# One expert weight loaded in four steps further back in the DMA queue, and 24 products of zeros in the TensorE order of a fused attention and mixture-of-experts kernel

## The chip, the cores and the metric

The kernel runs on one NeuronCore of a Trainium2 chip. The metric is the device time of one execution in microseconds (us); lower is better. One execution was also recorded by the hardware profiler.

## The reference

Three stages follow each other. The first is an attention over 4 batches, 8 heads, 576 tokens and 64 numbers per head; heads 0 to 3 see a local window of 32 tokens, heads 4 to 7 a stride of 32. The second sends each token to one of 8 experts (two matrix products each); whether a token takes a fresh expert or that of the token before it is decided by a gate. The third is a mixture of 4 causal attentions.

```python
# stage 1, per head
mask_local = (rel >= 0) & (rel < 32)
mask_strided = (rel >= 0) & (pos[None, :] % 32 == pos[:, None] % 32)
attn = softmax(where(mask, q @ k.T / 8, -1e9));  x = attn @ v
# stage 2, per token s
e = argmax(x @ w_gate) if s == 0 or sigmoid(x @ w_local) < 0.5 else prev_e
x = softmax(x @ w_gate)[e] * (relu(x @ w1[e]) @ w2[e])
# stage 3
out = sum over the top 2 of 4 experts of w * (softmax(causal(q @ k.T / 8)) @ v) @ wo
```

## The kernel before, in words

The change lies in the first attention, the first 130 us of some 586. Its work is cut into 16 units: unit `n` is batch `n // 4` and head pair `n % 4` (pairs 0 and 1 local, 2 and 3 strided). A unit passes through these steps:

- `load_qk(b, a)` and `load_vl` / `load_vs` (L223, L238, L243): DMA loads of queries, keys and values, all issued by SyncE (SP). Each of the nine `load_vl(b, t)` brings the local values of one stretch of tokens; it writes over the batch before, and so waits for that batch's last product with them.
- `prep` (L342): TensorE transposes `raw` into one of four rotating PSUM banks (`bank`, tag `t`), ScalarE copies it out as `ql`, `kl`, `qs`, `ks`.
- `s_mm` (L367): scores into the one PSUM tile `s`; VectorE takes the maximum (L391) and subtracts it (L397), which frees `s` for the next unit; ScalarE takes the exponential (L398).
- `et`, `pv`, `xt` (L403, L425, L465): transposes of the exponentials, product with the values, transposes of the result. `logits` and `route...` then choose the experts, batch by batch.

Beside it the weights of expert 0 are prepared: `load_w1(0)` (L159) issues four DMAs of 512 KB into `w1raw`, and sixteen `split_w1` (L165) each cut a quarter of one of the four pieces into a high part (ScalarE, L118) and a low part (VectorE, L119). They are first used by `h_early`, at the very end of this stage. `xt_early(r)` transposes rows of routed tokens that GpSimd gathers (`gather`, L187, tile `xg`).

The order is a list. `ev` collects the steps, each with a due time; it is sorted by due time and then traversed in the order of the index list `ORD`. TensorE executes exactly in that order (`manual_schedule`). SP's DMAs come out in that order too (so they stand in the trace). The orders of ScalarE, VectorE and GpSimd are made when the program is built, by a scheduler that starts an instruction when its own estimate of times says its inputs are there; every engine then executes its own list strictly in order.

`warm(n)` (L714) issues `n` products of a tile of zeros, `wz`, into a rotating bank that nobody reads; the kernel has one call of it, `warm(14)`, before the first step. `wz` shares its memory (tag `ess`, one buffer) with the strided units' exponentials.

Around the places that change the order is, before:

```python
# prep(0,1,1,0)  s_mm(1)  prep(0,2,0,0)  prep(0,2,0,1)  prep(0,3,1,1) ...
# load_qk(2,3)  s_mm(6)  load_qk(2,2)  ...  logits(0)  load_w1(0)  ...  pv(5)
# load_vl(2,0)  load_vl(2,7)  load_vl(2,2) ... load_vl(2,8) ... load_vl(2,6) ...
# s_mm(7) prep(2,0,1,0) prep(2,3,0,0) pv(6,0) prep(2,0,0,1) prep(2,2,1,0) ...
# load_qk(3,0) ... load_vs(2,2) ... load_vs(2,3) ... load_qk(3,1)
# pv(15,0)  et(15,1)  gather(0)  xt_early(0)  ...  xt_early(1)  ...  h_early(0)
```

Of the kernel before, what the change touches and what calls it, by code (L numbers as in the profile page):

```python
# [11 lines left out]
BF = mybir.dt.bfloat16  # L12
# [19 lines left out]
TAB = [{'et': [[[2.950979077143747, 3.950979077143747], [2.280661623723043, 3.280661623723043], [2.0962247253607327, 2.822324310858445], [2.6, 3.6], [2.6, 3.6]], [[3.5322171299090326, 4.532217129909033], [2.6, 3.6], [4.889421810674059, 5], [4.101973494858811, 5], [2.4273110594636376, 3.4273110594636376]]], 'pv': [[11.653333607501414, 13.276081673478151], [12.552811228649597, 12.274068241409006]], 'out': [27.06785727905669, 26.413251600982292, 31.393508979283784, 31.29028612353765, 33.51756297275431], 'load': 3.2539096467048427, 'fill': [-0.0001, 0.0, 2.2, 3.2, 3.8000000000000003, 4.7, 5.6000000000000005, 7.123278008936126, 7.475699072531977, 8.299999999999999, 9.28929322986803, 10.1, 11.279614409352465, 11.740498658223936, 13.41245718764738, 13.869517990637926, 14.180425775785736, 14.180525775785735, 16.109400886459948], 'ord': [[0, 1, 2, 3, 4], [4, 1, 3, 2, 0]]}, {'et': [[[2.6, 3.6], [0.4005259343533014, 1.4005259343533014], [2.7601240952552226, 3.7601240952552226], [1.8795577765734173, 2.8795577765734173], [4.194527945253478, 5]], [[3.136537199573193, 4.136537199573193], [2.570838837611794, 3.570838837611794], [3.583354236171958, 4.5833542361719575], [2.6, 3.6], [2.6, 3.6]]], 'pv': [[12.13577290663916, 14.511270833899513], [12.55, 12.576465944615482]], 'out': [24.42, 25.42, 27.908127481497882, 27.42, 28.42], 'load': 4.3618195128701025, 'fill': [0.2, 0.4539916075210759, 0.4540916075210759, 0.4541916075210759, 3.8000000000000003, 7.0225821487593425, 7.022682148759342, 7.022782148759342, 7.4, 8.299999999999999, 9.2, 10.1, 11.0, 11.9, 12.799999999999999, 13.60305564719335, 13.60315564719335, 13.60325564719335, 14.503255647193349], 'ord': [[0, 1, 2, 3, 4], [0, 1, 2, 3, 4]]}]  # L32
ORD = [5, 2, 0, 4, 7, 1, 3, 8, 10, 6, 16, 11, 12, 22, 19, 14, 20, 13, 17, 9, 18, 21, 24, 25, 26, 23, 29, 27, 15, 31,
# [12 lines left out]
NORM = [[[0, 1], [0, 0]], [[1, 0], [0, 0]], [[0, 1], [0, 0]], [[0, 1], [0, 0]], [[0, 0], [1, 1]]]  # L46

EE = ["avava", "vavav"]
# [8 lines left out]
def kernel(  # L57
# [18 lines left out]
    B, H, S, D = q.shape  # L76
# [16 lines left out]
    def pool(c, name, bufs=1, **kw):  # L93
        return c.enter_context(tc.tile_pool(name=name, bufs=bufs, **kw))
# [61 lines left out]
    wpool = pool(wctx, "wts")  # L156
    RAW1, RAW2, W1, W2 = {}, {}, {}, {}

    def load_w1(e):  # L159
        for c in range(4):  # L160
            t = wpool.tile([128, F], FT, name="w1raw", bufs=4)
            nc.sync.dma_start(t, moe_w1[e, c * 128:(c + 1) * 128, :])
            RAW1[e, c] = t
# [23 lines left out]
    def gather(e, rs=range(RC), rows=NT):  # L187
        for r in rs:
            t = wpool.tile([128, DM], FT, name="xg", bufs=6)
            nc.gpsimd.indirect_dma_start(out=t, out_offset=None, in_=xd[:rows],  # L190
                                         in_offset=bass.IndirectOffsetOnAxis(ap=gidx[:, r, e:e + 1], axis=0))
            XG[e, r] = t
# [10 lines left out]
    wk = pool(actx, "awk")  # L203
    ac = pool(actx, "acst")
# [8 lines left out]
    SL = (15.59, 17.66, 17.67, 17.5)  # L213
# [32 lines left out]
                nc.sync.dma_start(vs[a - LOC][64 * g:64 * g + 36, h, :, :64],  # L246
                                  dap(v, ((b * H + 2 * a + h) * S + 8 * g) * D, [[16 * D, 36], [D, 8], [1, D]]))

    wz = wk.tile([128, 512], BF, name="wz", tag="ess", bufs=1)
    nc.vector.memset(wz, 0.0)  # L250
    load_qk(0, 0)
    load_qk(0, 1)
# [148 lines left out]
    ess = {}  # L401
# [320 lines left out]
    ev = [(-9, prep, (0, a, x, hf)) for a in range(LOC) for x in range(2) for hf in range(2)]  # L722
# [26 lines left out]
    for b in range(B):  # L749
# [2 lines left out]
        r = [(logits, (b, (0, 1))), (logits, (b, (2, 3)))]  # L752
        r += [(f, (b,)) for f in (route0, route1, route_w, route2, route2b, route3, route3b, route_r, route4)]
        ev += [(o + x, *y) for x, y in zip(t, r)]
    ev += [(SL[0], slots, (slice(0, 2), slice(0, 1), lambda: gather(0, [0, 1], (B - 1) * S))), (6, load_w1, (0,))]
    for c in range(4):
        for i in range(4):
            ev.append((7.66 + W1S * (4 * c + i), split_w1, (0, c, 4, i)))
# [4 lines left out]
           (SL[2], slots, (slice(0, RC), slice(1, NE), lambda: gather(1)))]  # L763
    for f in range(8):
        ev += [(HE[f], h_early, (f,)), (YT_[f], y_early, (f,))]
    ev.sort(key=lambda x: x[0])
    for i in ORD or range(len(ev)):
        ev[i][1](*ev[i][2])
# [306 lines left out]
    def next_w(e, r):  # L1075
        for c in range(4):
            if c % RC == r or (r == 0 and c == 3):
                split_w1(e, c)

    load_w1(1)  # L1080

    ov = cst.tile([128, 4, NE], FT)
# [39 lines left out]
    xt_expert(1)  # L1122
    tc_m = ExitStack()
    load_w1(2)
    tc_m.enter_context(tc.manual_schedule(engines={mybir.EngineType.PE, mybir.EngineType.Pool}))
    load_cn(1)
# [263 lines left out]
    def qk_steps(b, pr):  # L1390
        return [(c_qk, (b, pr, n, hf)) for n in range(2) for hf in range(2)]
# [8 lines left out]
    ev = [(-4, c_t, (0, 4))] + [(-3, f, a) for f, a in qk_steps(0, 0)] + [(-2, c_v, (0, t)) for t in range(5)] + [(-1, c_top2, (0,))]  # L1400
# [54 lines left out]
```

## Time and profile before

| | us |
|---|---|
| median of 3 runs | 589.42 (586.23 to 590.1) |
| the profiled execution | 587.65 |
| its span, first to last instruction | 585.6 |
| TensorE busy | 553.1 (94% of the span) |
| VectorE busy | 383.3 (65%) |
| ScalarE busy | 348.0 (59%) |
| mean granted TensorE clock | 0.981 |

The device time holds 2.05 us beside the span. PE is TensorE's matmuls and transposes, PEld its weight loads (they overlap), DVE is VectorE, ACT ScalarE, POOL GpSimd, SP SyncE; SPq is SP's queue of DMA issues. L347 is line 347 of the kernel. The granted clock is a share of 2.4 GHz: 1.00 is the full level, 0.50 the lower one, 1.2 GHz. "Issue" as the end of a wait means that the profile shows nothing for which the engine waited.

### The profile page before, as it was taken

The numbers are of one execution on the slowest core, as the hardware profiler recorded it, in microseconds if no ns is written. First come the engines' busy times: TensorE is split into PE (matmuls) and PEld (weight loads), VectorE is DVE, ScalarE is ACT, GpSimd is POOL, SyncE is SP. The second block draws the span as 40 slices with busy tenths as digits, with TensorE's granted clock in tenths as the row PEclk, the third lists the DMA queues.
The fourth block names the chain that finished last, engine by engine and source line by source line (L and its number), as shares of the span: only waits on it lengthen the run. The fifth ranks groups of instructions, "written<-read, shape, count | busy, mean of one in ns | idle before, by whom it ended". The sixth has DMA issues, their size and how long they took to land. (4 is left out here: it accounts for less than half of the span.)

```text
span 585.6 us, 14138 instructions
## 1 busy us (share of the span) xinstructions
PE 553.1 (94%) x5207; PEld 478.4 (82%) x5207; DVE 383.3 (65%) x1145; ACT 348.0 (59%) x865; POOL 142.4 (24%) x231
## 2 busy tenths in 40 slices
PE   5999899879998999999999999998999999999996
PEld 3777778668778898988989987797987999889764
DVE  4356588855573646474747476157998888798892
ACT  4566676741373544564646467245877876776882
POOL 6032213250431432423443453220000001000000
PEclk9799699989999999999999999999999999999999
DMA  9999969640584764275837360324103402301312
GB/s 180 188 245 230 257 168 225 208 152 0 176 293 150 222 219 167 84 213 194 261 135 256 126 211 21 100 79 119 36 11 73 162 3 58 82 34 42 103 31 90
DMA packets 81127, 82.01 MB, mean 140 GB/s; under 512 B 56840, under 2 KB 57096, under 8 KB 80528
## 3 DMA queue, kind: packets, MB, share of 16 engines
q1 hardware_dynamic: 72768, 64.92, 39.7%
q0 software_dynamic: 8112, 15.76, 8.4%
q8 instruction: 59, 0.97, 0.7%
q14 instruction: 28, 0.23, 0.1%
q10 hardware_dynamic: 160, 0.13, 0.1%
HBM read 61.89 MB, written 21.76 MB: 143 GB/s over the span
## 5 line engine op out<-in xcount | busy, mean ns | idle before, releaser
L196 POOL DMA_INDIRECT yd<-y,sidx x47 | 51.2, 1089 | 91.7 <-ACT y L974 54.4
L1275 ACT ACTIVATE E<-cs,c_mx 128x288 f32<-128x288 f32 (+4 forms) x96 | 45.7, 481 | 13.8 <-DVE c_mx L1273 6.5
L122 PE MATMUL yp<-w2h,h 128*128 128x512 f32 x128 | 51.1, 399 | 0.1
L119 DVE TENSOR_TENSOR w1l<-w1raw,w1h 128x1024 fp32r<-128x1024 f32 (+1 forms) x44 | 41.5, 981 | 14.0 <-ACT w1h L118 14.0
L124 PE MATMUL yp<-w2h,h 128*128 128x512 f32 x128 | 50.0, 390 | 0.0
L123 PE MATMUL yp<-w2l,h 128*128 128x512 f32 x128 | 49.9, 390 | 0.0
L119 DVE TENSOR_TENSOR w2l<-w2raw,w2h 128x512 fp32r<-128x512 f32 x56 | 35.7, 685 | 19.2 <-ACT w2h L118 18.6
L118 ACT ACTIVATE w1h<-w1raw 128x1024 fp32r<-128x1024 f32 (+1 forms) x44 | 33.8, 832 | 19.7 <-PE hp L123 19.7
L1305 POOL MEMSET E<- 128x128 f32 x40 | 8.2, 210 | 145.9 <-PE cet L1324 69.7
L710 DVE SCALAR_TENSOR_TENSOR h<-hp,h 128x384 fp32r<-128x384 f32 x48 | 24.7, 551 | 28.8 <-ACT h L709 22.5
L118 ACT ACTIVATE w2h<-w2raw 128x512 fp32r<-128x512 f32 x56 | 31.8, 632 | 19.2 <-PE yp L124 8.2
L1268 PE MATMUL cs<-qkt 128*128 128x288 f32 (+4 forms) x192 | 39.1, 319 | 0.5 <-DVE qkt L1198 0.5
L1273 DVE TENSOR_REDUCE c_mx<-cs 128x1 f32<-128x288 f32 (+4 forms) x80 | 37.8, 483 | 1.7 <-PE cs L1268 1.0
L122 PE MATMUL qkp<-y,cw 128*128 128x288 f32 x128 | 38.7, 303 | 0.0
L124 PE MATMUL qkp<-y,cw 128*128 128x288 f32 x128 | 37.7, 295 | 0.0
L123 PE MATMUL qkp<-y,cw 128*128 128x288 f32 x128 | 37.6, 294 | 0.0
L709 ACT ACTIVATE h<-hp 128x384 fp32r<-128x384 f32 x48 | 21.4, 489 | 20.8 <-PE hp L124 13.5
L122 PE MATMUL hp<-xo,w1h 128*128 128x320 f32 (+2 forms) x96 | 30.5, 318 | 1.5 <-issue 1.5
L190 POOL DMA_INDIRECT xg<-xd,gidx x24 | 25.2, 1052 | 26.2 <-DVE gidx L653 19.2
L1319 PE MATMUL cet<-idf,E 128*128 128x128 f32 x160 | 28.2, 278 | 2.4 <-ACT et L115 0.8
L124 PE MATMUL hp<-xo,w1l 128*128 128x320 f32 (+2 forms) x96 | 30.1, 314 | 0.0
L123 PE MATMUL hp<-xo,w1h 128*128 128x320 f32 (+2 forms) x96 | 30.1, 314 | 0.0
(372 smaller groups left out, 1675.8 us busy)
## 6 DMA issues: line engine op xcount, KB each, us to landing
w1raw<-in_moe_w_dram SPq DMA_DIRECT2D x32, 512.0 KB
w2raw<-in_moe_w_dram SPq DMA_DIRECT2D x56, 256.0 KB
qkt<-qkt SPq DMA_DIRECT2D x8, 576.0 KB
yr<-yd SPq DMA_DIRECT2D x16, 256.0 KB
out_dram<-co SPq DMA_DIRECT2D x16, 256.0 KB
raw<-in_q_dram SPq DMA_DIRECT2D x16, 144.0 KB
raw<-in_k_dram SPq DMA_DIRECT2D x16, 144.0 KB
raw<-in_q_dram SPq DMA_DIRECT2D x8, 288.0 KB
```

The source lines that it names most:

```text
L118: nc.scalar.activation(hi, src, AF.Copy)
L119: (eng or nc.vector).tensor_tensor(lo, src, hi.bitcast(FT), op=OP.subtract)
L122: nc.tensor.matmul(o, ah, bh, start=start, stop=False, **kw)
L123: nc.tensor.matmul(o, ah, bl, start=False, stop=False, **kw)
L124: nc.tensor.matmul(o, al, bh, start=False, stop=stop, **kw)
L190: nc.gpsimd.indirect_dma_start(out=t, out_offset=None, in_=xd[:rows], in_offset=bass.IndirectOffsetOnAxis(ap=gidx[:, r, e:e + 1], axis=0))
L196: nc.gpsimd.indirect_dma_start(out=yds[n], out_offset=bass.IndirectOffsetOnAxis(ap=ix(n), axis=0), in_=y, in_offset=None, bounds_check=yds ...
L710: nc.vector.scalar_tensor_tensor(lo, p, 0.0, hi.bitcast(FT), op0=OP.max, op1=OP.subtract)
L1268: nc.tensor.matmul(o[:, h - h0], T[:, h, q0:q0 + 128], T[:, 2 + 2 * x + h, k0:k1], start=x == 0, stop=x == 1, skip_group_check=True)
L1273: nc.vector.tensor_reduce(mx[:, n, h0:h0 + G], o, axis=AX.X, op=OP.max, negate=True)
L1275: nc.scalar.activation(E[:, h, k0:k1], o[:, h - h0], AF.Exp, bias=mx[:, n, h:h + 1], accum_out=sm[:, n, h:h + 1])
L1319: nc.tensor.transpose(p[:, kt * 128:kt * 128 + 128], E[:, kt * 128:kt * 128 + 128], idf)
```

## The change

Three things are changed.

- `load_w1(0)`, one step that issued all four DMAs, becomes four steps of one DMA each. They stand further back: the first behind `load_vl(2,8)`, the second behind `load_vl(2,6)` (the last of the third batch's local values), the third behind `load_qk(3,0)`, the fourth behind `load_vs(2,3)`. `load_qk(2,2)`, which stood ahead of the weight, goes behind `load_vl(2,0)` and `load_vl(2,7)`.
- Four calls of `warm` are put into the order: `warm(10)` ahead of `s_mm(1)`, `warm(5)` behind it, `warm(3)` between `pv(15,0)` and `et(15,1)`, `warm(6)` ahead of `xt_early(0)`.
- `wz` gets memory of its own, since it is now read through the whole stage.

All other steps keep their places relative to each other; the index list is longer because the step list is.

```diff
-    def load_w1(e):
-        for c in range(4):
+    def load_w1(e, cs=range(4)):
+        for c in cs:
...
-    wz = wk.tile([128, 512], BF, name="wz", tag="ess", bufs=1)
+    wz = ac.tile([128, 512], BF, name="wz")
...
-    ev += [(SL[0], slots, (slice(0, 2), slice(0, 1), lambda: gather(0, [0, 1], (B - 1) * S))), (6, load_w1, (0,))]
+    ev += [(SL[0], slots, (slice(0, 2), slice(0, 1), lambda: gather(0, [0, 1], (B - 1) * S)))]
+    ev += [(6 + c * .01, load_w1, (0, (c,))) for c in range(4)]
...
+    ev += [(0, warm, (10,)), (0, warm, (5,)), (0, warm, (3,)), (0, warm, (6,))]
```

The four places in the order after, with new steps in angle brackets:

```python
# prep(0,1,1,0)  <warm(10)>  s_mm(1)  <warm(5)>  prep(0,2,0,0) ...
# load_vl(2,0)  load_vl(2,7)  <load_qk(2,2)>  load_vl(2,2) ... load_vl(2,8)
# <load_w1 0>  load_vl(2,6)  <load_w1 1>  load_qk(3,0)  <load_w1 2>
# load_vs(2,2)  load_vs(2,3)  <load_w1 3>
# pv(15,0)  <warm(3)>  et(15,1)  gather(0)  <warm(6)>  xt_early(0)
```

## Rows read from the trace of the kernel before

**Rows 1.** The page: span, and TensorE's busy time, share and instructions.
```profile
span 585.6 us, 14138 instructions
...
PE   553.1 (94%) x5207; PEld 478.4 (82%) x5207; DVE 383.3 (65%) x1145; ACT 348.0 (59%) x865; POOL 142.4 (24%) x231
```
**Rows 2.** Windows: length, busy us of PE, PEld, DVE, ACT, POOL; clock, DMA share, GB/s.
```profile
320.00:340.00 20.00, 20.00 (x140) 18.19 (x139) 10.97 (x19) 10.59 (x20) 9.24 (x9) 1.00 0.43 146
```
**Rows 3.** Windows, as in rows 2: a stretch at the lower clock.
```profile
22.00:23.00 1.00, 1.00 (x10) 1.00 (x9) 0.00 (x0) 0.85 (x3) 0.00 (x0) 0.50 0.80 167
```
**Rows 4.** Timeline of PE, first units: start, us, ..., what ended the idle time.
```profile
14.31 0.98 PE L374 MATMUL s<-ml,idb 128*128 128x480 bf16 x2 [2.93 <-DVE z L397]
...
17.03 1.03 PE L347 MATMUL prep<-idf,raw 72*128 72x72 f32 x8
19.36 0.97 PE L347 MATMUL prep<-idf,raw 72*128 72x72 f32 x12 [1.30 <-DMA raw<-in_k_dram]
```
**Rows 5.** Timeline of PE, around the longest wait.
```profile
56.72 0.56 PE L452 MATMUL pv<-vs,ess 64*64 64x65 f32 x18
60.67 0.70 PE L452 MATMUL pv<-vs,ess 64*36 64x65 f32 x14 [3.39 <-issue]
61.30 2.18 PE L347 MATMUL prep<-idf,raw 96*128 96x96 f32 x14
63.41 1.14 PE L452 MATMUL pv<-vs,ess 64*64 64x65 f32 x32
64.48 0.18 PE L560 MATMUL pk<-idb,r_row 5*128 5x5 bf16 x1
...
68.98 0.60 PE L474 MATMUL xt<-idf,xr 128*128 128x128 f32 x4
```
**Rows 6.** Windows, as in rows 2: a wait with its fall of the clock.
```profile
59.00:60.00 1.00, 0.00 (x0) 0.00 (x0) 0.00 (x0) 0.00 (x0) 0.00 (x0) 0.50 1.02 397
```
**Rows 7.** Timeline of PE: steps of the same form at the full clock.
```profile
36.57 0.89 PE L379 MATMUL s<-kl,ql 64*64 64x96 f32 x31 [0.59 <-issue]
37.39 0.72 PE L347 MATMUL prep<-idf,raw 96*128 96x96 f32 x7
37.95 0.51 PE L481 MATMUL xt<-idf,xs 100*128 100x100 f32 x4
...
39.23 0.69 PE L452 MATMUL pv<-vs,ess 64*64 64x65 f32 x32
39.85 0.72 PE L347 MATMUL prep<-idf,raw 96*128 96x96 f32 x7
```
**Rows 8.** DMA queues in 34.0:34.1: packets, MB, share of 16 engines.
```profile
q8 instruction: 1, 0.02, 64.7%
```
**Rows 9.** DMA queues in 58.0:58.1.
```profile
q8 instruction: 1, 0.02, 71.6%
```
**Rows 10.** Timeline of SPq: DMA issues.
```profile
11.48 0.39 SPq L230 DMA_DIRECT2D raw<-in_k_dram  x1
...
49.70 3.10 SPq L162 DMA_DIRECT2D w1raw<-in_moe_w_dram  x4
53.36 0.59 SPq L240 DMA_DIRECT2D vla<-in_v_dram  x1
...
78.14 0.48 SPq L230 DMA_DIRECT2D raw<-in_q_dram  x1
```
**Rows 11.** Windows, as in rows 2: the last load of rows 10 runs out.
```profile
83.00:84.00 1.00, 1.00 (x15) 0.94 (x11) 0.86 (x6) 0.56 (x3) 0.00 (x0) 1.00 0.52 133
```
**Rows 12.** Timeline of PEld: weight loads of the products of zeros.
```profile
3.73 0.15 PEld L717 LDWEIGHTS <-wz 128*128 128x128 bf16 x1 [0.28 <-issue]
4.11 1.18 PEld L717 LDWEIGHTS <-wz 128*128 128x128 bf16 x6 [0.23 <-issue]
```
**Rows 13.** Timeline of PE: the end of the first attention.
```profile
127.82 0.63 PE L671 MATMUL xpe<-idf,xg 128*128 128x128 f32 x4 [1.27 <-DMA xg<-xd,gidx]
```
**Rows 14.** Waits of ACT in 0:180.
```profile
ACT w2s L118 <- DMA w2e<-in_moe_w_dram: 0.9, 1, 0.9
```

More of the change, by code (lines that the diff above doesn't have):

```diff
@@ L32 @@
 TAB = [{'et': [[[2.950979077143747, 3.950979077143747], [2.280661623723043, 3.280661623723043], [2.0962247253607327, 2.822324310858445], [2.6, 3.6], [2.6, 3.6]], [[3.5322171299090326, 4.532217129909033], [2.6, 3.6], [4.889421810674059, 5], [4.101973494858811, 5], [2.4273110594636376, 3.4273110594636376]]], 'pv': [[11.653333607501414, 13.276081673478151], [12.552811228649597, 12.274068241409006]], 'out': [27.06785727905669, 26.413251600982292, 31.393508979283784, 31.29028612353765, 33.51756297275431], 'load': 3.2539096467048427, 'fill': [-0.0001, 0.0, 2.2, 3.2, 3.8000000000000003, 4.7, 5.6000000000000005, 7.123278008936126, 7.475699072531977, 8.299999999999999, 9.28929322986803, 10.1, 11.279614409352465, 11.740498658223936, 13.41245718764738, 13.869517990637926, 14.180425775785736, 14.180525775785735, 16.109400886459948], 'ord': [[0, 1, 2, 3, 4], [4, 1, 3, 2, 0]]}, {'et': [[[2.6, 3.6], [0.4005259343533014, 1.4005259343533014], [2.7601240952552226, 3.7601240952552226], [1.8795577765734173, 2.8795577765734173], [4.194527945253478, 5]], [[3.136537199573193, 4.136537199573193], [2.570838837611794, 3.570838837611794], [3.583354236171958, 4.5833542361719575], [2.6, 3.6], [2.6, 3.6]]], 'pv': [[12.13577290663916, 14.511270833899513], [12.55, 12.576465944615482]], 'out': [24.42, 25.42, 27.908127481497882, 27.42, 28.42], 'load': 4.3618195128701025, 'fill': [0.2, 0.4539916075210759, 0.4540916075210759, 0.4541916075210759, 3.8000000000000003, 7.0225821487593425, 7.022682148759342, 7.022782148759342, 7.4, 8.299999999999999, 9.2, 10.1, 11.0, 11.9, 12.799999999999999, 13.60305564719335, 13.60315564719335, 13.60325564719335, 14.503255647193349], 'ord': [[0, 1, 2, 3, 4], [0, 1, 2, 3, 4]]}]
-ORD = [5, 2, 0, 4, 7, 1, 3, 8, 10, 6, 16, 11, 12, 22, 19, 14, 20, 13, 17, 9, 18, 21, 24, 25, 26, 23, 29, 27, 15, 31,
[12 rows of a table removed]
+ORD = [5, 2, 0, 4, 7, 1, 3, 8, 10, 6, 11, 20, 12, 15, 16, 26, 23, 18, 24, 17, 21, 9, 22, 25, 28, 29, 30, 27, 33, 31,
[12 rows of a table added]
 NORM = [[[0, 1], [0, 0]], [[1, 0], [0, 0]], [[0, 1], [0, 0]], [[0, 1], [0, 0]], [[0, 0], [1, 1]]]
```

24 rows, old and new, of the table ORD are left out of this document.

## The prediction

> **What bounds the kernel now.** First the page: TensorE is busy in 94% of the span [rows 1]. Then the windows of 20 us: in the later stages it is busy in 20.00 of 20 us at the full clock [rows 2], so what is lost or gained before them is carried to the end; only the first 130 us have holes. There the windows of 1 us show where the clock stands at its lower level (one row stands for such stretches around 14 to 18, 21 to 25, 59 to 69 and 120 to 124 us) [rows 3], and TensorE's timeline shows the waits ahead of them: 2.93 us until VectorE has freed the score bank, 1.30 us for a load of keys [rows 4], and 3.39 us in the middle of one `pv`, where nothing that the profile shows is waited for [rows 5]. The clock falls inside that last wait [rows 6] and stays down until about 69 us.
>
> The costliest place is thus 57.28 (60.67 less 3.39) to 69 us. What ends that wait? A second "issue" wait, of 0.59 us, ends at 36.57 [rows 7]. In both cases the instruction queue q8 starts a block of 0.02 MB shortly before, at 34.0 [rows 8] and at 58.0 [rows 9]: TensorE goes on 2.6 and 2.7 us after these starts. So I read the 3.39 us as a wait for TensorE's own code. And the block started late in a stretch full of `w1raw`: its four DMAs (2 MB) were issued from 49.70 to 52.8 [rows 10], and at 59 to 60 us the queues still move 397 GB/s at a DMA share of 1.02 [rows 6].
>
> **The change part by part.**
>
> *The weight leaves 49.70 us.* If the code block no longer stands among 2 MB, the 3.39 us go: -3.4. Each piece now is 512 KB, 1.3 us at the 397 GB/s of [rows 6]; what could be left of a code wait lies between nothing and the 0.59 us of [rows 7], seen among small loads. I take nothing, since a piece is a quarter of the load that stood there.
>
> *The clock behind it.* Without the wait nothing makes it fall there. From 60.67 to 68.98, 8.31 us ran at the lower level. Equal work at both levels: fourteen transposes 2.11 us (61.30 to 63.41) against twice 0.56 (37.39 to 37.95), a ratio of 0.53; 32 products of `pv` 1.07 us (63.41 to 64.48) against 0.62 (39.23 to 39.85), 0.58 [rows 5, 7]. At their mean, 0.555, the 8.31 us become 4.6: -3.7.
>
> *What is late next: `load_qk(2,2)`.* It moves from ahead of the weight to behind `load_vl(2,0)` and `load_vl(2,7)`. The first of these waits for `pv(5)` and was issued at 53.36 for 0.59 us [rows 10]; one more like it, and the two DMAs of `load_qk(2,2)` (288 KB each) go out at about 54.4 and 54.8. TensorE needs the keys at 57.28 plus the rest of `pv(6,0)` (14/32 of 0.62, so 0.27) plus three transposes (3/7 of 0.56, so 0.24): 57.8. When do they land? Three DMAs of this form were issued from 78.14 on [rows 10] and the queue ran out about halfway through the window 83:84 [rows 11], some 5.5 us for three, so 4.0 for two: 58.4, a wait of 0.6. At the other end, the keys of unit 3 were issued at 11.48 and ended TensorE's wait at 19.36, 7.9 us later [rows 10, 4]: 62.7, a wait of 4.9. The second had nine loads of small pieces ahead of it, the first hardly any; here there are two, and GpSimd's writes of results beside them. Nearer to the first: +1.1.
>
> *The four pieces at their new places.* SP's queue is in order: `load_vl(2,6)`, `load_qk(3,0)`, `load_vs(2,2)`, `load_vs(2,3)` and what follows them come behind one to four pieces of 1.3 us each. Between 28 and 127 us no wait of TensorE ends with a DMA, and the DMAs ahead of them lose 2 MB; nothing. The sixteen splits stay the same instructions, later; they are needed at 130 us. ScalarE (59% busy) and VectorE (65%) [rows 1] must take them in the gaps of 70 to 90 us; nothing, unless a split stands in front of a load that has not landed (third rival).
>
> *`warm(10)`, in the 2.93 us wait of `s_mm(1)`.* A product costs 0.43 us at the lower level (0.15 of weight load and 0.28 before it) and about 0.2 at the full one (six weight loads in 1.18) [rows 12]. The clock is full at 11.38, so 10 products end at 13.5, ahead of 14.31: free. No clock falls then during `s_mm(1)`, whose 2.72 us (14.31 to 17.03) [rows 4] become 1.6, 1.1 us less. But the keys that end the next wait at 19.36 come no earlier; only ScalarE's exponential of this unit, and the copies behind it, move forward. Between nothing and 1.1, the middle: -0.6. *`warm(5)`* runs from 15.9 to 17.0 in the room that this makes: free. Before 22 us [rows 3] TensorE only waits and transposes, as it will after, so I leave that stretch of 3.3 us at the lower level; were it gone too, 0.45 of 3 us, 1.3, would come on top.
>
> *`warm(3)` and `warm(6)`* stand in front of `et(15,1)` and `xt_early(0)`. Neither waited before; the clock was still low until 123.7, when the first three start. Three at about 0.35 and six at 0.2 are 2.3 us (bounds: nine at 0.22 and at 0.43, 2.0 and 3.9). The next wait behind them, for the gathered rows at 127.82, is 1.27 us [rows 13] and takes that much; no clock fell in it. Net +1.0 (between 0.7 and 2.6; nothing if the rows come later).
>
> *`wz` in its own memory* costs no instruction; the exponentials that shared it no longer wait for it, and did not visibly before.
>
> **Sum.** -3.4 - 3.7 + 1.1 - 0.6 + 1.0 = -5.6. The profiled execution took 587.65 us (span 585.6 and 2.05 around it): 582.05, so 582.1. That execution is 1.8 us under the median of the three runs, 589.42; from the median the same sum would give 583.8.
>
> **The rivals.**
>
> *First: the long wait is not the weight's doing, and stays.* The trace never says for what TensorE waited, and the second wait of this kind, at 36 us, arose without any `w1raw` [rows 7, 8]. Then only the products count: 587.65 - 0.6 + 1.0 = 588.05. For it speaks a missing row; against it, that in fast stretches of equal length with small loads only 0.59 us were lost. The Trainium skill speaks for it: its page "Runtime: NRT & Kernel Launch", section "Instruction fetch mechanics", has the code fetched ahead in blocks, with the cost of crossing a block's end "mostly hidden". By that rule the 3.39 us could hardly be code at all; the two waits that end 2.6 and 2.7 us after a block starts say otherwise.
>
> *Second: a wait for the moved load takes its place.* Price at the late end: 4.9 us in place of 3.4, with the same fall of the clock, so +1.5 and no gain of 3.7: 587.65 + 1.5 - 0.6 + 1.0 = 589.6. It decides from a wait of about 3 us on, where the clock has fallen twice [rows 4, 6]; in the 1.27 us of [rows 13] it did not.
>
> *Third, on the other side: the splits block ScalarE.* Its order is fixed when the program is built, from estimated landing times; a split placed ahead of its piece's landing holds the exponentials and bank copies behind it, and with four banks TensorE stops soon after. In this trace the only such wait at a like load is 0.9 us [rows 14]; `w1raw` itself was split 14 us after its issue. The gain is used up when the four pieces block for 1.4 us each (5.6); at 3.4 each, as long as TensorE's longest wait, the time is 582.05 + 13.6 = 595.7.
>
> **How the numbers follow.** Forecast 0.63, first rival 0.15, second 0.14, third 0.08. The forecast's own range goes from 578.5 (no wait for the moved load, 1.1 from `s_mm(1)`, nothing lost at the end, some of the 1.3) to 585.5 (a wait of 3 us with the clock kept, and the upper end at the last products). 578.5 to 589.6 takes in both middle rivals and leaves out the third. One per cent, about what a measurement can tell here, is 5.9 us: faster means below 583.5, slower above 595.3. Of the forecast's 0.63 I put 0.48 below 583.5 and 0.15 above; with the first two rivals and half of the third, the same is 0.48; slower 0.04.
>
> **What would show it.** Right: no "issue" wait over 1 us near 57 us, a granted clock of 1.00 from 50 to 100 us, `s_mm(1)` in 1.6 us, and a wait of about 1 us for `raw` ahead of the transposes of unit (2,2). Wrong: that wait at 3 us or more and the clock at 0.50 behind it; ScalarE's waits naming DMA `w1raw`; a code block that starts late among the pieces; a time between 130 us and the end that is not as long as before, since the orders of the other engines are made anew.

## The result, and the profile after

The change brought no time. Two sets of runs were made, each beside runs of the kernel before. In the first the kernel after had a median of 592.49 us (587.58 to 596.73, 16 runs) against 588.88, a ratio of 1.0062 with a 95% interval of 1.0032 to 1.0091. In the second it had 588.35 us (585.0 to 593.93, 12 runs) against 589.57: 0.9999 (0.9964 to 1.0034). Both lie within 1%. The forecast was 582.1 us, a ratio of 0.99. The ratios leave out executions that took over 1.5% more than the fastest of the same kernel, and the times in the profiles of such executions (those of e2, e7 and e13, below) are not compared. The executions of one kernel spread over some 10 us, and one profile is one draw from that spread; so two profiles of the kernel after are read here, of an execution of 592.56 us in the first set and, further down, of one in the second.

The page of the first, as in [rows 1]:

```profile
span 590.7 us, 14187 instructions
...
PE   561.1 (95%) x5231; PEld 482.4 (82%) x5231; DVE 384.2 (65%) x1145; ACT 349.6 (59%) x865; POOL 143.4 (24%) x231
```

The span is 5.1 us longer. TensorE is busy for 8.0 us more, and 24 products account for some 6 of them. The timeline of PE at the places of [rows 4], [rows 7], [rows 5] and [rows 13], and at two waits near 80 us (start, us, what; in brackets the idle time ahead and what ended it):

```profile
14.33 0.58 PE L374 MATMUL s<-ml,idb 128*128 128x480 bf16 x2 [0.61 <-DVE z L397]
...
15.83 1.25 PE L717 MATMUL wm<-wz 128*128 128x512 bf16 x5
...
32.93 0.57 PE L452 MATMUL pv<-vs,ess 64*64 64x65 f32 x23 [0.18 <-DVE xs L459]
35.96 0.49 PE L452 MATMUL pv<-vs,ess 64*36 64x65 f32 x9 [2.46 <-issue]
...
63.07 0.69 PE L452 MATMUL pv<-vs,ess 64*64 64x65 f32 x32
63.69 0.47 PE L347 MATMUL prep<-idf,raw 96*128 96x96 f32 x3
66.03 1.39 PE L347 MATMUL prep<-idf,raw 72*128 72x72 f32 x11 [1.88 <-DMA raw<-in_k_dram]
...
79.78 0.54 PE L481 MATMUL xt<-idf,xs 100*128 100x100 f32 x4 [0.90 <-DVE xs L459]
...
86.68 0.42 PE L414 MATMUL et<-idf,z 128*96 128x128 f32 x2 [0.39 <-DVE slot_acc L643]
...
134.00 0.63 PE L671 MATMUL xpe<-idf,xg 128*128 128x128 f32 x4 [1.73 <-DMA xg<-xd,gidx]
```

Three things are to be seen first. `s_mm(1)` takes 1.5 us (14.33 to 15.83), where it took 2.72. The `pv` that held the 3.39 us of [rows 5] runs through as 32 products at 63.07. But two waits have grown: the "issue" wait near 36 us from 0.59 to 2.46, and in front of the keys of `load_qk(2,2)` a new one of 1.88. Behind both, and behind the wait for gathered rows at the end, the clock is low (windows: busy us of PE, PEld, DVE, ACT, POOL; clock, DMA share, GB/s):

```profile
36.00:37.00 1.00, 1.00 (x13) 0.88 (x13) 0.41 (x2) 0.00 (x0) 0.00 (x0) 0.50 0.78 238
69.00:70.00 1.00, 1.00 (x18) 0.68 (x20) 0.92 (x4) 0.00 (x0) 0.18 (x1) 0.50 0.98 324
135.00:136.00 1.00, 1.00 (x15) 0.63 (x18) 0.69 (x1) 0.86 (x2) 0.00 (x0) 0.50 0.20 70
```

Windows of 1 us show it low for 13.6 us from 35 on, 6.8 from 66 on and 3.4 from 134 on; the spells of before at 14 to 18, 21 to 25 and 120 to 124 us are gone. Where the time went is best told by the starts of `s_mm(n)`, after less before: -1.3 us at `s_mm(3)`, +6.4 at `s_mm(5)` (the wait at 36 us and its spell), +3.9 at `s_mm(8)` (2.4 us gained over the place of the long wait, where 7.1 less 1.1 were forecast), +6.6 at `h_early(0)`. Of these, 1.5 us come back later. The two waits for VectorE near 80 us are taken up further down.

### The profile page after: what moved, and what is told of

Same layout as the page of the kernel before. It is cut to its first block, busy times and chain, and to the rows that moved or that the text cites. A ratio compares the mean times of both kernels' runs of the same rounds, so it can differ in the third digit from the quotient of the medians.

```text
span 590.7 us, 14187 instructions
## 1 busy us (share of the span) xinstructions
PE 561.1 (95%) x5231; PEld 482.4 (82%) x5231; DVE 384.2 (65%) x1145; ACT 349.6 (59%) x865; POOL 143.4 (24%) x231
## 5 line engine op out<-in xcount | busy, mean ns | idle before, releaser
L1277 ACT ACTIVATE E<-cs,c_mx 128x288 f32<-128x288 f32 (+4 forms) x96 | 45.8, 482 | 13.7 <-DVE c_mx L1275 6.5
L347 PE MATMUL prep<-idf,raw 72*128 72x72 f32 (+1 forms) x224 | 26.8, 259 | 6.1 <-DMA raw<-in_k_dram 4.6
```

The source lines that it names most:

```text
L347: nc.tensor.transpose(p[:, i, :], raw[a][:n, x, hf * 3 + i].rearrange("p h d -> p (h d)") if loc else raw[a][:n, x, hf, i * 128:i * 128 + ...
L1277: nc.scalar.activation(E[:, h, k0:k1], o[:, h - h0], AF.Exp, bias=mx[:, n, h:h + 1], accum_out=sm[:, n, h:h + 1])
```

## The experiments

Each kernel is the kernel after (e15: the kernel before) but for the edit shown, and each ratio is to the kernel before on the same chip. The table takes the starts from one profile of each: "low" is the time at the lower clock before 160 us (1-us windows, summed as twice what the granted clock lacks of 1), "(3,1)" the first DMA of `load_qk(3,1)`. The rows of e2, e7 and e13 have the ratio alone; e14 and e15 are told in the text.

| kernel | ratio (95%) | low | `s_mm(9)` | (3,1) | `s_mm(11)` | `h_early` | span |
|---|---|---|---|---|---|---|---|
| before | 1 | 20.5 | 73.06 | 74.78 | 87.39 | 130.1 | 585.6 |
| after | 1.0062 (1.0032 to 1.0091) | 23.8 | 77.31 | 79.94 | 92.77 | 136.7 | 590.7 |
| e1 loads alone | 0.9997 (0.9961 to 1.0033) | 30.7 | 76.94 | 80.55 | 92.39 | 137.3 | 592.0 |
| e2 zeros alone | 0.9952 (0.9917 to 0.9986) | | | | | | |
| e3 loads, 15 tiny products | 0.9973 (0.9945 to 1.0) | 13.6 | 70.90 | 75.39 | 86.68 | 130.3 | 584.8 |
| e4 weight alone | 0.9987 (0.9952 to 1.0023) | 17.1 | 67.41 | 74.55 | 85.58 | 130.2 | 585.0 |
| e5 after, `load_qk(2,2)` back | 0.9967 (0.993 to 1.0004) | 10.2 | 70.38 | 74.12 | 85.84 | 129.8 | 584.1 |
| e6 after, early zeros only | 0.9954 (0.9917 to 0.999) | 6.8 | 69.35 | 74.55 | 85.56 | 128.3 | 580.4 |
| e7 after, late zeros only | 1.0011 (0.9981 to 1.0042) | | | | | | |
| e8 after, 24 tiny products | 0.9967 (0.9931 to 1.0002) | 13.6 | 72.00 | 75.95 | 87.44 | 131.0 | 584.2 |
| e9 after again | 0.9999 (0.9964 to 1.0034) | 13.6 | 71.57 | 75.90 | 87.02 | 131.4 | 585.8 |
| e10 weight, early zeros | 0.9989 (0.9952 to 1.0025) | 13.7 | 68.41 | 75.04 | 88.62 | 132.3 | 585.9 |
| e11 early zeros alone | 0.9976 (0.9942 to 1.001) | 20.5 | 75.56 | 77.41 | 89.95 | 134.2 | 587.1 |
| e12 after, 48 tiny products | 1.0008 (0.9971 to 1.0045) | 17.1 | 76.08 | 81.61 | 93.68 | 137.3 | 591.9 |
| e13 zeros in the third batch | 0.9978 (0.9937 to 1.0018) | | | | | | |
| e16 zeros at the gather | 0.9971 (0.9929 to 1.0013) | 23.8 | 79.34 | 82.04 | 94.79 | 138.4 | 591.4 |
| e17 weight late, early zeros | 0.9923 (0.9881 to 0.9965) | 10.2 | 70.22 | 71.98 | 84.21 | 130.7 | 585.0 |
| e18 weight late, no zeros | 0.9953 (0.9922 to 0.9984) | 13.6 | 67.54 | 69.33 | 81.57 | 127.5 | 584.6 |

**The parts, each without the others.** e1 has no added zeros; e2 has the zeros and the loads in their old order; e3 is e1 with fifteen products of one column behind `warm(14)`, where TensorE waits for its first load; e4 is e1 with `load_qk(2,2)` back at its place, so that only the weight has moved.

```diff
-    ev += [(0, warm, (10,)), (0, warm, (5,)), (0, warm, (3,)), (0, warm, (6,))]     # e1, e3, e4
+    warm(14);  pad(15)                                                               # e3
-    load_vl(2,0)  load_vl(2,7)  load_qk(2,2)                                         # e4
+    s_mm(6)  load_qk(2,2)  ...  load_vl(2,0)  load_vl(2,7)                           # e4
```

> The load parts of the change alone (weight in four steps, load_qk(2,2) moved), no added product of zeros. Theory (the added products of zeros make TensorE run out of its code at 33.5 us, 2.46 us long, and the clock falls behind it): the issue wait near 36 us is back at about 0.6 us and the clock stays full from 36 to 50 us; the issue wait near 57 us (3.4) is gone; a wait of about 2 us for raw_k of unit (2,2) with a shorter spell at the lower clock stays. Time about 2.4 us under the kernel before (the gain between units 7 and 8 of the changed kernel's trace), 586.5. Rival (the moved loads, not the zeros, make the kernel slower): 590 or more, long wait near 36 us still there.

> The 24 products of zeros alone, the loads in the order of the kernel before. Theory: the issue wait of about 2.5 us at 33.5 to 36 us and the spell of about 13 us at the lower clock behind it are there, as in the changed kernel; the wait near 57 us may be there as well, since the weight stands in one block of 2 MB again. Time about 592 to 596, slower than the changed kernel. Rival (loads are to blame): like the kernel before or up to 1.3 us faster, 587 to 589.

> The load parts alone, and 15 products of one column each behind the first 14 products of zeros, in the wait for the first loads: as many TensorE instructions as the first two calls add, at almost no time, and no work in the waits at 11 and 16 us. If the end of a code block, moved 15 products forward, is what lengthens the wait near 36 us: an issue wait of about 1.7 us (0.6 and 16 instruction pairs earlier, 1.1 us) near 35 us, and perhaps the fall of the clock, 588 to 593. If it is TensorE's being 1.3 us early: a wait of 0.6 us or none, as with the load parts alone, 586.5.

> The weight in four steps, load_qk(2,2) left at its old place ahead of the third batch's local values, no added products. Theory: neither the code wait near 57 us nor the wait for raw_k of unit (2,2): the whole of 3.4 and 3.7 us is gained, clock full from 36 to 115 us, 588.9 - 7 = 582. Rival (the 3.4 us wait is not the weight's doing): the wait near 57 us is there, 588 to 589.

No part costs anything by itself. The loads alone earn nothing that these runs can tell (e1 and e4), where 6 us or more were forecast; the zeros alone earn 0.5% (e2), where a loss of 0.4 us was. The code wait near 57 us belongs to the weight: with the old loads (before, e2, e11) it is there, with moved ones (after, e1, e3, e4 and every later kernel) no more than 0.22 us of it is left (e10). The timeline of PE in e11, the same `pv` as in [rows 5]:

```profile
60.19 0.33 PE L452 MATMUL pv<-vs,ess 64*64 64x65 f32 x2
63.54 1.13 PE L452 MATMUL pv<-vs,ess 64*36 64x65 f32 x30 [3.03 <-issue]
```

e4 is the telling one: it has the forecast gain at this place, with `s_mm(9)` 5.65 us ahead of before, and has lost it again at `h_early`, 130.2 against 130.1.

**After, less one part.** e5 puts `load_qk(2,2)` back, e6 and e7 take away the late and the early zeros, e8 adds 24 tiny products at the start.

```diff
+    s_mm(6)  load_qk(2,2)                                  # e5
+    warm 10, 5, 0, 0                                       # e6
+    warm 0, 0, 3, 6                                        # e7
+    warm(14);  pad(24)                                     # e8
```

> The kernel after with load_qk(2,2) alone put back behind s_mm(6), ahead of the four pieces; all 24 zeros stay. Moved-load theory: the 1.88 us wait for raw at 66 us and the lower clock behind it are what the two parts together cost; about 1% under the kernel after, ratio to before 0.993 to 0.998. Shifted-block theory (15 added products let a block of TensorE's code end in the quick pv products near 33.5 us, 2.46 us of wait and 13 us at the lower clock): that stall stays, ratio 1.003 or more, and in the profile an issue wait of over 2 us near 36 us. Late-zeros theory (warm(3), warm(6) and the gather behind them): also 1.003 or more.

> The kernel after with warm(10) and warm(5) alone, warm(3) and warm(6) left out. Shifted-block theory: the stall near 36 us stays, ratio 1.003 to 1.008. Late-zeros theory: the loss is gone, 0.995 to 1.0. In the profile the late-zeros theory wants no clock fall between 125 and 140 us; the shifted-block theory makes no claim there.

> The kernel after with warm(3) and warm(6) alone, warm(10) and warm(5) left out. Shifted-block theory: the block ends where it did before, the issue wait near 36 us is 0.4 to 1.4 us, ratio 0.995 to 1.001. Late-zeros theory: ratio 1.003 to 1.008.

> The kernel after with 24 products of one column added behind warm(14), where TensorE waits for the first load: they take no time of their own, but every block of TensorE's code ends 24 pairs of instructions earlier in the program. Shifted-block theory: the issue waits change size and place all along; the stall near 33.5 to 36 us moves ahead of that pv and is under 1.5 us, and the time falls by 2 us or more from the kernel after (ratio 0.995 to 1.002). Moved-load and late-zeros theories: no change against the kernel after, ratio 1.003 to 1.009.

Read against the first set's 1.0062, each of the four looks like a cure, which no single cause explains. The next run shows why.

**After once more, and three mixtures.** e10 is the kernel after with `load_qk(2,2)` back and early zeros only, e11 early zeros on the old loads, e12 has 48 tiny products.

> The kernel after, unchanged, once more. Two readings of its first profile are told apart. Fixed-place reading: its waits are those of the program (blocks of code end at fixed instructions), so another execution shows the same 2 to 3 us issue wait near 36 us, the raw wait near 66 us and about 24 us at the lower clock before 160 us; ratio 1.003 to 1.009. Draw reading: each execution hits other waits, lower-clock time before 160 us comes out anywhere from 7 to 30 us and the span follows it with about 0.53 us per us; ratio anywhere from 0.996 to 1.003.

> The weight in four steps, load_qk(2,2) at its old place, warm(10) and warm(5), no late zeros: each part that came out well alone. If the parts add: ratio 0.990 to 0.994 (582 to 585 us). If TensorE merely runs ahead into the loads of the third batch (as where load_qk(2,2) alone was put back: 2.41 us of wait for raw at 52 us): 0.995 to 1.0, with a wait for raw of over 2 us between 50 and 62 us.

> The loads as before, warm(10) and warm(5) alone: what the early zeros are worth by themselves. Worked out from the two lower-clock spells of before at 14 to 18 and 21 to 25 us that they end (3.4 us each, 0.445 of it lost): 3.0 us, ratio 0.995. If the time is lost again at the next late load or block of code: 0.998 to 1.002.

> The kernel after with 48 products of one column behind warm(14), 1.5 us in a wait for the first load: blocks of code end 48 pairs earlier than in the kernel after, 24 earlier than in the kernel with 24 such products. Fixed-place reading: other issue waits again, and a time that differs from the kernel after by its stall near 36 us (ratio 0.995 to 1.0). Rival, that the products do something else than shift (clock, start): the same as with 24 of them or a loss of up to 1 us against it.

Neither reading of e9 was right as it stood: the code wait near 34 us keeps its place in the program and changes its size, and the wait for `raw` comes at another load. The timeline of PE in e9, where the same 23 and 9 products stand as in the first profile of the kernel after, and the wait for `raw` that this time comes at 53 us:

```profile
32.33 0.57 PE L452 MATMUL pv<-vs,ess 64*64 64x65 f32 x23
33.95 0.34 PE L452 MATMUL pv<-vs,ess 64*36 64x65 f32 x9 [1.04 <-issue]
...
53.32 0.71 PE L347 MATMUL prep<-idf,raw 96*128 96x96 f32 x3 [2.72 <-DMA raw<-in_q_dram]
```

The starts of e9 less those of before are -2.0 us at `s_mm(3)`, -1.5 at `s_mm(5)`, +3.7 at `s_mm(7)` (the wait at 53 us and its spell), +0.1 at `s_mm(8)` and +1.3 at `h_early(0)`: the same program loses its time at another place.

A block of code for TensorE starts at 31.1 us here and at 33.1 in the first profile, and TensorE goes on 2.85 and 2.86 us later; so in these two the wait is long where the block starts late against TensorE's arrival. The 1.0 us wait had no fall of the clock behind it, the 2.46 us wait one of 13.6 us. Over the table, the span follows the time at the lower clock: a line through the 15 profiles has 0.45 us of span for each us (correlation 0.83), about the 0.445 that the prediction took. These are 14 programs beside before, though, and between the executions of one program the slope is smaller. With the time at the lower clock worked out from each execution's span and mean granted clock, it is 0.34 us for each us over the 15 executions of the kernel after in the first set, 0.27 over the 32 of before in the second, and none over the twelve of e3. Nor does it tell the two kernels apart: in the second set the kernel after ran for 14.5 us at the lower clock on average and before for 23.2, and their times are equal. What the kernel after saves there, it loses in waits. e12 gives no support to a shift as a remedy: 48 tiny products bring 1.0008, with an interval that overlaps that of the 24 in e8.

**Filling the waits, and taking traffic away.** e13 moves the late zeros, ten each, ahead of the two waits of the third batch; e16 has eight in front of `xt_early(1)` in place of three ahead of `et(15,1)`; e14 and e15 are the kernels after and before without the loads of one batch's values.

```diff
+    <warm(10)> prep(2,1,0,0)   <warm(10)> prep(2,2,1,0)    # e13, none at the end
+    <warm(6)> xt_early(0)      <warm(8)> xt_early(1)       # e16
     def load_vl(b, t):                                     # e14, e15; load_vs alike
+        if b == 1: return
```

> The kernel after, its two late groups of zeros moved: ten products each in front of prep(2,1,0,0) and prep(2,2,1,0), where executions so far waited 2.4 to 3.9 us for raw and the clock fell for 6.8 to 10.2 us; none at the end of the stage. Clock theory: where zeros fill the wait, 2.2 us at the full level, the granted clock stays 1.00 from 50 to 70 us; a spell of 6.8 us not had is worth 3.0 us, less up to 2.2 us for the group that meets no wait: ratio 0.990 to 0.999. Load theory (the loads set the time there, the clock is a side effect): unit 8 starts as late as before, 64 to 65 us, and the ratio is 0.998 to 1.005 though the clock is held.

> The kernel after with its three products ahead of et(15,1) taken away and eight put in front of xt_early(1), where TensorE waits 1.4 to 2.1 us for gathered rows and the clock falls for 3.4 us in most executions. Clock theory: the wait is filled, no fall between 125 and 140 us, 1.5 us less for the fall and 0.8 us less for the three products: 0.996 of the kernel after, ratio to before 0.994 to 0.999. If the rows set the time: no change against the kernel after, and h_early starts no earlier behind xt_early(1).

> The kernel after with the loads of the second batch's values (load_vl and load_vs of batch 1, 1.2 MB in pieces of 256 bytes) left out; the batch is worked out with the first batch's values. If the waits for code near 34 us and for raw at 53 to 66 us come from the traffic of these small pieces on the DMA queues: the issue wait near 34 us is under 0.6 us, the raw wait at 53 us is gone, unit 8 starts before 61 us, ratio to before 0.988 to 0.993. If a block of code takes its 2.6 us whatever the traffic is: the issue wait stays at 1 to 2.5 us, ratio 0.995 to 1.003.

> The kernel before with the same loads left out. Traffic theory: with room on the queues the change earns what was forecast, so this kernel is 3 to 5.6 us slower than the kernel after without these loads, ratio about 0.998. If the change earns nothing in any case: both come out within 2 us.

In e16 the clock is full from 130 to 140 us, with TensorE busy for 8.96 of the 10 us. The windows of e13 show TensorE busy and the clock full through the stretch in which the kernel after waited:

```profile
50.00:70.00 20.00, 20.00 (x431) 15.01 (x426) 11.53 (x36) 10.22 (x27) 5.12 (x8) 1.00 0.79 204
```

Neither brought time that their executions show. So the clock can be held through one stretch without a gain that can be told; that what TensorE waits for comes no sooner is the likely reason, but only argued, and the same profile of e13 has the clock low at other places (88 to 93 and 133 to 140 us). In e14 the wait for code near 34 us stayed (1.91 us, its block started at 31.7), so that wait does not hang on these 1.2 MB; the DMA share there was still 1.0 to 1.15. The waits for `raw` between 20 and 127 us were gone. Their ratios to before, 1.0445 (1.0389 to 1.0501) and 1.0488 (1.0419 to 1.0557), lie in the forecast's direction, but overlap; the time on top comes behind 130 us (`h_early` starts at 130.3 and 132.7), probably because other values send tokens to other experts. In both, routing (`ACT lts`, 3.3 to 3.5 us) held TensorE at 55 us, and in e15 the code wait near 57 us is not seen behind it; so they say little about the rest.

**The weight out of the busy stretch.** The table shows a part of what caps the gain. With the old loads (before, e11) `load_qk(3,1)` goes out 1.7 and 1.9 us behind the start of `s_mm(9)`; with the four pieces at their new places it is 2.6 to 7.1 us, the most where TensorE is earliest (e4, e10). In eight of the profiles ahead of e17 it goes out between 74.1 and 76.0 us, though `s_mm(9)` starts anywhere from 67.4 to 73.1; and `s_mm(11)`, which comes behind its transposes, never started before 85.5. In e3, e10 and e12 TensorE waits 0.3 to 2.4 us for these keys. In e4 and e6 it waits 1.38 and 0.71 us at the same transposes, and the profile names instructions of ScalarE (`w1h`, `r_nf`) whose results a transpose of `raw` does not read. Their keys had been issued 6.5 and 7.2 us before, so the keys are the likelier reason; that is argued. In the other six with the pieces there (after, e1, e5, e8, e9, e16) no wait at this place ends with a load. The windows of 64 to 80 us in before and e4:

```profile
64.00:80.00 16.00, 15.53 (x334) 12.71 (x328) 14.47 (x52) 13.65 (x35) 3.96 (x6) 0.85 0.93 192
...
64.00:80.00 16.00, 14.42 (x322) 12.24 (x320) 13.72 (x47) 13.32 (x34) 2.55 (x4) 0.89 1.06 237
```

In before the queues have room (0.43 at 72 to 74 us), and SP waits 2.5 us for a `pv`, so TensorE sets the pace; in e4 and e10 the DMA share is above 1 (1.06 and 1.09), also at 72 to 74 (1.05 and 1.14), and SP's longest wait for TensorE is 0.6 us. e10 meets it head on, with keys that were issued at 76.06:

```profile
83.50 1.20 PE L347 MATMUL prep<-idf,raw 96*128 96x96 f32 x6 [2.41 <-DMA raw<-in_k_dram]
```

A second loss does not hang on the keys. From `s_mm(9)` to `s_mm(11)` TensorE takes 14.3 and 14.4 us in before and e11, but 15.44 to 15.46 in the six kernels without a wait for keys. Of these 1.1 us, 0.84 are in the two waits for VectorE near 80 us: the one for `xs` is 0.45 us in before and 0.90 in after, the one for `slot_acc` is new with 0.39. VectorE's list has splits of the weight there, and one of them stood for 0.83 us until ScalarE had written its high part, with the maximum of `s` and `slot_acc` behind it. The wait for `xs` in before (PE), and the split ahead of `slot_acc` in after (VectorE):

```profile
75.08 0.54 PE L481 MATMUL xt<-idf,xs 100*128 100x100 f32 x4 [0.45 <-DVE xs L459]
...
85.31 0.43 DVE L119 TENSOR_TENSOR w1l<-w1raw,w1h 128x256 fp32r<-128x256 f32 x1 [0.83 <-ACT w1h L118]
```

e17 (on e10) and e18 (on e4) therefore load the weight a batch later, with its first four splits behind it.

```diff
-    load_vl(2,8) <load_w1 0> load_vl(2,6) <load_w1 1> load_qk(3,0) <load_w1 2> ... load_vs(2,3) <load_w1 3>
+    load_qk(3,1) <load_w1 0> ... load_vl(3,4) <load_w1 1> ... load_qk(3,2) <load_w1 2> ... load_vl(3,8) <load_w1 3>
```

> load_qk(2,2) at its old place, warm(10) and warm(5), and the four pieces of the weight a batch later: behind load_qk(3,1), load_vl(3,4), load_qk(3,2) and load_vl(3,8), the first four splits behind them. Queue theory (the DMA engines are the bound of 56 to 80 us once TensorE is ahead: share 0.98 to 1.37 without a gap, and load_qk(3,1) goes out at 74.5 to 76 us in nine kernels however early TensorE is): without 2 MB there, some 5 us at 390 GB/s, load_qk(3,1) goes out before 73 us, s_mm(11) starts before 84 us (85.6 at best so far, 87.39 before), the stage ends before 128 us; ratio 0.990 to 0.995. If something else holds TensorE there (ScalarE, routing): s_mm(11) no earlier than 85.5 us, ratio 0.996 to 1.001.

> The same without any added zeros, so the kernel before with its weight loaded a batch later. Queue theory: load_qk(3,1) goes out when TensorE frees its buffers and no later; the gap of 3.4 us from the code wait near 57 us with its clock, forecast at 7.1 us, now stays: s_mm(11) before 85 us, ratio 0.991 to 0.996. If something else holds TensorE: 0.998 to 1.002.

Both are faster than the kernel before, by 0.8% and 0.5% (e2 and e6 are the only others whose interval ends below 1). The two sets of the kernel after came out 0.6% apart, so one set at 0.5% proves little; the 0.8% of e17 is the most that any kernel here had. e18's windows, and the transposes that e10 had to wait for, now without a wait:

```profile
64.00:80.00 16.00, 15.63 (x362) 13.16 (x363) 12.22 (x45) 11.77 (x30) 3.19 (x5) 1.00 0.82 211
...
78.72 0.71 PE L347 MATMUL prep<-idf,raw 96*128 96x96 f32 x6
```

`load_qk(3,1)` goes out at 71.98 and 69.33, 1.8 us behind `s_mm(9)` in both, and `s_mm(11)` starts at 84.21 and 81.57, 14.0 us behind `s_mm(9)`. This is one profile of each, and the pieces and the first splits left together, so keys and splits are not told apart. The details were not all as expected: 84.21 misses "before 84" by little, and e17's stage ends at 130.7, not before 128; between 84 and 104 us TensorE is busy for 17.35 and 16.84 us of 20, where before had 18.62, with the splits now in that stretch (ScalarE is busy for 14.39 and 14.70 us instead of 12.82); both have a new wait of 1.20 us for VectorE behind `s_mm(11)`. In e18 `h_early` comes 2.7 us sooner than in before, and the span is only 1.0 us shorter. Between e17 and e18 the measurement does not choose, nor between them and e6 (0.9954).

## Why the prediction was wrong, point by point

**The wait near 57 us (-3.4): right.** It left with the weight and stayed with it, in every kernel but e15. The first rival (the weight has nothing to do with it) falls. The reason is in part argued. In before, the block started at 58.0, after TensorE had stopped at 57.28, and at 58 to 60 us the queues carried 385 GB/s at a share of 1.01; in after a block starts at 59.3 and is there before TensorE needs it at 63.1, with 142 GB/s at 0.41. That the 2 MB delay the block is likely, but no run shows it apart from other traffic; in e4 the block starts at 54.1, with the share at 0.93 and 225 GB/s from 54 to 56 us, and is there before TensorE needs it at 56.85. The Trainium skill's "mostly hidden" ("Runtime: NRT & Kernel Launch", section "Instruction fetch mechanics") holds for this block and fails for those near 34 us, whose waits of 0.54 to 3.21 us stand in nine profiles at the same product of the same `pv`.

**The clock behind it (-3.7): the size was right, the saving did not come.** What failed is "without the wait nothing makes it fall there": in both profiles of the kernel after it is low in that stretch all the same, for 6.8 and 10.2 us, behind a wait for `raw`.

**The wait for the moved load (+1.1): mis-sized, and its decision point too.** SP issued the first of its two DMAs 3.2 us ahead of TensorE's need (60.93 and 64.15), close to the 3.4 forecast; until both had landed it took 5.1 us instead of 4.0. So the wait was 1.88 us, and 1.8 to 3.8 in e1, e3, e6, e8, e12 and e16. The second rival put the point from which it decides at 3 us; the clock fell at 1.88, and the prediction's own rows already had it low at 21 to 25 us, behind the wait of 1.30 us. In e9 TensorE was held at 53 us by another load of the batch, ahead of which no piece of the weight had gone out.

**`warm(10)` and `warm(5)` (-0.6): right as far as they reach.** `s_mm(1)` took 1.5 us, forecast 1.6, and the two early spells went, which the text had as a bonus of 1.3; `s_mm(3)` came 1.3 us sooner in one profile of the kernel after and 2.0 in the other, more than the 0.6 forecast. They do not go always: e12 and e16 wait 4.28 and 2.55 us for keys near 20 us and have the second spell. What the forecast missed is that fifteen more products move the end of every later block of code. The one near 36 us now ends among quick products of `pv`, 23 of 32 through, and the text had left that wait at its 0.59. At the old place it was 0.47 to 1.34 us (before, e1, e4, e18), at the new one 0.54 to 3.21 in nine profiles, with 1.54 in the middle. In the first profile this one place cost 7.7 us (from -1.3 to +6.4).

**`warm(3)` and `warm(6)` (+1.0): the products as forecast, the wait not.** They took 0.8 and 1.3 us, but the wait for gathered rows behind them did not shrink by as much as they took; it grew, to 1.73 and 2.10 us from 1.27, and now the clock fell for 3.4 us. So nothing was there to set against their 2.1 us.

**"The four pieces at their new places ... nothing" and "what is lost or gained before them is carried to the end": the steps that failed the sum.** The prediction rests them on TensorE: busy in 94% of the span, and no wait of it between 28 and 127 us ends with a DMA. That is so in before, where TensorE is late; it does not say how soon the loads could come. The queues are as full up to 80 us, 0.97 in 56 to 80 us before, and 2 MB whose first piece goes out some 12 to 16 us later (49.70 before, 61.55 and 65.58 after) stay within that stretch. Once TensorE is early, it meets loads: `raw` at 52 to 53 us in e5 and e9 (2.41 and 2.72 us), where it was some 2 us early, and the keys of `load_qk(3,1)`, behind the fourth piece, in e3, e10 and e12 (0.3 to 2.4 us) and probably in e4 and e6. The splits, put at nothing as well, cost time too: 0.84 us of waits for VectorE between `s_mm(9)` and `s_mm(11)`, also where no keys are waited for. Of 5.65 us gained in e4, 1.8 were left at `s_mm(11)` (a code wait of 0.68 us and a fall of the clock at 72 to 77 us have a share in it) and none at the end. With the weight out of the stretch `s_mm(11)` started 1.3 us (e17) and 4.0 us (e18) sooner than the 85.56 that was the earliest until then; but of e18's 5.8 us against before, 2.7 were left at `h_early` and 1.0 at the end. The Trainium skill's page "DMA: Bandwidth & Descriptors", section "Why small descriptors are slow (HBM only)", gives 256-byte pieces an overhead of 27%; the rows agree in kind: 226 GB/s at a share of 0.97 in 20 to 40 us of before, where the attention's small pieces run, and 385 at 1.01 in 58 to 60 us, where the weight does.

**The third rival** (splits block ScalarE) came, but small and by way of VectorE: not 1.4 to 3.4 us for each piece, but the 0.84 us above, where the split in VectorE's list waits for ScalarE.

**`wz` in its own memory** stands in every kernel here but before and e15 and was not tried by itself; e1 and e4, which have it without added zeros, gain nothing by it.

What stays open: what decides when a block of code starts, how the loss behind `s_mm(9)` divides between keys and splits, and whether the kernel after is truly slower than before by up to 0.6% or equal, since its two sets differ.

## What to carry to other kernels

A share of busy time over a whole span hides which engine binds a stretch: look at the DMA share of the very stretch where time is to be gained, and ask which load the faster engine will meet next. The transfer moved within a stretch whose queues are full earned nothing here (1.0062 and 0.9999); moved out of it, it did better (0.9923 and 0.9953). The work that hangs on a transfer moves with it, and costs time where it stands in front of what the bounding engine needs. And where executions of one kernel differ by 10 us, a wait in one profile is a draw: repeat the profile of the same program before a cause is read from the difference of two.

## What the runs showed of the hardware that was not expected

- The same wait for code, at the same instruction of one `pv`, was 0.54 to 3.21 us in nine executions. In four of them (1.04 in e9, 1.91 in e14, 2.46 in after, 3.21 in e17) the start of the block's transfer is known; from it to TensorE's next product it was 2.76 to 2.86 us in all four. In e17 the block started at 33.8 us, after TensorE had reached its end at 33.35:

```profile
q8 instruction: 1, 0.02, 74.6%
...
36.56 0.49 PE L452 MATMUL pv<-vs,ess 64*36 64x65 f32 x9 [3.21 <-issue]
```

- The fall of the clock behind such a wait is not of one size: nothing at 1.04 us, 13.6 us of it behind 2.46, 6.8 behind 3.21. In e6 a wait of 0.94 us had 3.4 us of it behind, in e11 one of 0.85 had 10.2.
- Products of zeros held the clock at 1.00 from 50 to 70 us in e13, and its executions show no gain for it (0.9978, 0.9937 to 1.0018).
